# First tokens of a fused Fourier mixer and MLP in another order, stores on GpSimd's queue, weight conversions rescheduled

## The chip, the cores and the metric

One core of a Trainium2 chip runs the whole kernel. The metric is device microseconds of one launch. Several executions are timed; their median counts. One more execution is profiled, and all rows below are from that one.

## The reference

`x` has 8 batches of 3072 positions and 256 channels. Each batch is mixed along its positions in the frequency domain, and the result goes through a two-layer MLP, all in float32:

```
X = rfft(x, axis=1)
Yr = Xr @ w_r - Xi @ w_i + b_r          # 256 x 256 weights
Yi = Xr @ w_i + Xi @ w_r + b_i
Y = soft_shrink(Yr, 0.01) + 1j * soft_shrink(Yi, 0.01)
x = irfft(Y, n=3072, axis=1).reshape(8 * 3072, 256)
h = x @ w_in                            # 256 x 2048
out = softplus(h) @ w_out               # 2048 x 256
```

## The kernel before

Large matmuls are made of three: every operand is split into a high and a low part in fp32r, and `mm3` (L207 to L210) adds high x high, high x low and low x high. A batch passes through these stages:

- `s1` (16 chunks c per batch): a short Fourier transform over 96 rows, psf, copied by ACT (L260). In the early part the chunks of batch 0 stay on the chip as `a0`; chunks of batch 1 go to DRAM (`a_dr`) and come back as `ap` (L273 to L276).
- `s3`, the mix and `s4` for 12 groups gp: the second transform (L287), the product with w_r and w_i (`wmh`, `wml`), bias and soft shrinkage on DVE and POOL (z, cl; L377 to L382), the first step back (L427), copied as `d` (L432) and stored to `d_dr`.
- `s5`: the last step of the inverse transform. The tokens come as four blocks (column block j, channel half k) from `dp`, which is read from `d_dr` (L440, L441). `b11`, `b21`, `b12`, `b22` make from them the seven left factors of a Strassen-like product (`whole`, `keep`, `difference`, `split_token`; L474 to L489).
- The MLP, by a key (batch, pair of blocks, slice m2 of the hidden units): seven products psc and pse by the seven combinations of `w_in`, sums on ACT and DVE (L532, L537), softplus (L543), splitting (L547, L553), and pso with `w_out`.

**Weights.** `w_in` and `w_out` arrive as 64-bit numbers. A generator `split_w` converts one piece j of 16 (load L143; L158 to L194 on ACT, DVE and POOL) and stores it to DRAM (L195), from where `stream_w` (L204) loads it for each key. A piece is spread over several steps, one part at each `yield`: L158 to L161 first, then L163 to L165, then the sum (L178 to L182), the cast L192, the low part L194 and the store. The pieces with `early` set that belong to `w_in` use a corner of the buffer `y1`; all others share one buffer, `wp` (`bufs=1`). So the next piece's L178 or L182 waits until the last store from `wp` has landed.

**Order.** The program is written out step by step. A list `first` gives the steps before zero (`early` is on): s1 of batch 0, the 12 groups with s1 of batch 1 in between, then six more s1 of batch 1 (c = 4 to 9), then four s5. From step 0 on there are four steps per key. `at(t, f, ...)` hangs a piece of work (a load, a conversion, an s1) on step t; `later` puts off something by one step, and `store` (L97) uses it. SyncE's queue (SP) issues nearly all DMAs in that order; one that has to wait holds all behind it. Buffers count: `x`, `xh`, `xl`, `a`, `d` and the streamed weights have two each, the early `xt` lie in the buffers of `gh` and `gl`.

What the change touches: `store` (L97), `load_w` (L137), `split_w` (L150 to L196), `load_x` (L225), `s1` (L240 to L264), `s5` (L445 to L462), `put_split` and `b12` to `b21` (L493 to L516), and the schedule (L646 to L718).

Of the kernel before, what the change touches and what calls it, by code (L numbers as in the profile page):

```python
# [10 lines left out]
F32 = mybir.dt.float32  # L11
# [3 lines left out]
ALU = mybir.AluOpType  # L15

B, S, D, DFF = 8, 3072, 256, 2048
P = 128
# [3 lines left out]
BLK = 512  # L22
# [11 lines left out]
def tile_spectral_mixer_mlp(ctx, tc, x, w_r, w_i, bias, bias_0, w_in, w_out, f, f_hi, f_lo, g1, g3, g3_hi, g3_lo, hm, out):  # L34
# [61 lines left out]

    def store(dst, src, what):  # L97

        def start():
            nc.sync.dma_start(dst, src)  # L100
            stored[what] += 1

        later.append(start)
# [33 lines left out]
    def load_w(which, m2):  # L137

        if m2 < 6:
            st = sb.tile([P, 1024 + 4 * N1], F32, tag="dp", name="w64", bufs=4)[:, :1024]  # L140
        else:
            st = sb.tile([P, 1024], F32, tag="w64", name="w64", bufs=1)
        nc.sync.dma_start(st.rearrange("p (a n) -> p a n", a=2).bitcast(U32), (w_in if which else w_out)[:, m2])  # L143
        stages[which, m2] = st

    def split_w(which, m2):
# [46 lines left out]
        yield  # L193
        v.tensor_tensor(out=lo, in0=src, in1=hi.bitcast(F32), op=ALU.subtract)  # L194
        nc.sync.dma_start((w1_dr if which else w2_dr)[m2][:, :], w.bitcast(F32))  # L195
        stored["w", which, m2] += 1  # L196
# [28 lines left out]
    def load_x(b, c):  # L225

        if b == 0 or (b, c // 10) == (1, 0):
            xt = sb.tile([P, 512], F32R, tag=("gh", "gl")[c % 2], name="xt", bufs=3).bitcast(F32)[:N1]
        else:
            xt = sb.tile([P, 512], F32, tag="x", name="xt", bufs=2)[:N1]  # L230
        nc.sync.dma_start(
            xt.rearrange("p (n c) -> p n c", n=2),
            x[b].rearrange("(p n) c -> p n c", n=N2)[:, 2 * c:2 * c + 2, :],
        )
        xs[b, c] = xt
# [7 lines left out]
    def s1(b, c):  # L243
# [17 lines left out]
        if b == 0:  # L261
            stored["a", b] += 1
        else:
            store(a_dr[b][:, 2 * c:2 * c + 2, :].rearrange("(g q) n c -> q g n c", q=4), a.rearrange("p (n c) -> p n c", n=2), ("a", b))  # L264

# [182 lines left out]
    def s5(b, blk, k):  # L448
# [3 lines left out]
        while t < (blk + 1) * BLK:  # L452
# [8 lines left out]
            t += n  # L461
        (b11, b21, b12, b22)[blk % 2 * 2 + k]((b, blk // 2), ps)  # L462

# [29 lines left out]
    def put_split(*args):  # L493
        split_token(*args) if early else later.append(lambda: split_token(*args))

# [7 lines left out]
    def b12(key, ps):  # L503
        difference(0, ps)
        keep(key, 1, ps)
        put_split(key, T1, 0, nc.vector if early else nc.gpsimd)

    def b22(key, ps):
        whole(key, B22, ps)
        difference(1, ps)  # L510
        difference(0, ps)
        put_split(key, T2, 0, nc.vector if early else nc.gpsimd)
        put_split(key, T3, 1, nc.vector)

    def b21(key, ps):
        whole(key, B21, ps)  # L516
        difference(0, ps)
        put_split(key, T4, 0, nc.vector if early else nc.gpsimd)

# [107 lines left out]
    with tc.manual_schedule():  # L627
# [17 lines left out]
        def plan_s1(b, start, step, first=0):  # L645
            for c in range(first, 16):  # L646
                t = product(start + step * (c - first), s1, b, c)
                at(t - 3, split_x, b, c)
                at(t - 7, load_x, b, c)

# [28 lines left out]

        first += [("s1", 1, c) for c in range(4, 10)]  # L680
        first += [("s5", j, k) for j, k in ((0, 0), (1, 0), (1, 1), (0, 1))]
        t0 = -len(first)
# [17 lines left out]
        for k in range(2):  # L700
            at(t0 + 14 + k, load_mix, k)
            at(t0 + 18 + k, split_mix, k)
        for j in range(NM):
            t = t0 + 23 + 5 * j if j < 9 else 1 + 3 * (j - 9)
            at(t - (6 if j < 9 else 4 if j < 12 else 2), load_w, (j + 1) % 2, j // 2)
            before.setdefault(t, []).append(split_w((j + 1) % 2, j // 2))
# [10 lines left out]
        nt = NT  # L717
        plan_s1(1, 1, 1.6, 10)  # L718
        for b in range(B):
# [135 lines left out]
```

## Time and profile before

| | |
|---|---|
| median of the runs | 2680.17 us |
| lowest and highest of 3 | 2677.96 and 2680.23 us |
| the profiled execution: its own time | 2679.82 us |
| its span in the trace | 2678.0 us |
| PE busy | 2603.8 us, 97% of the span |
| DVE, ACT, POOL busy | 61%, 64%, 11% |
| mean granted clock of TensorE | 0.987 |

The span is what the trace covers; 1.8 us of the profiled execution's time lie around it. Shares are means over the whole span, most of which is the steady part from step 24 on. What differs is the start, so the sections below look at stretches of the first 250 us. Lines (L195) are those of the code printed above; `w_dr` in the trace stands for the arrays `w1_dr` and `w2_dr`, `w` for several weight tiles, and `a_dr<-y` for the early chunks of batch 1 that are kept in `y1`.

### The profile page before, as it was taken

How to read it: one execution, taken by the hardware profiler on the slowest of the kernel's cores; microseconds unless marked ns; L12 is line 12 of the kernel's file. 1: busy time of each engine (PE TensorE's matmuls, PEld its weight loads, DVE VectorE, ACT ScalarE, POOL GpSimd, SP SyncE). 2: the span in 40 equal slices, each digit the busy share in tenths (PEclk: the TensorE clock that was granted, in tenths of full speed). 3: DMA queues.
4: the chain of work that ended last, by engine and by line, in shares of the span. 5: the costliest groups of instructions: out<-in, count | busy, mean ns of one | idle time of the engine just before them, and what ended most of it. 6: DMA issues, size and time to landing. Idle time of an engine off the chain costs nothing.

```text
span 2678.0 us, 36264 instructions
## 1 busy us (share of the span) xinstructions
PE 2603.8 (97%) x13059; PEld 2184.2 (82%) x13059; DVE 1626.2 (61%) x2701; ACT 1719.5 (64%) x3115; POOL 301.3 (11%) x292
## 2 busy tenths in 40 slices
PE   7768999999999999999999999999999999999999
PEld 5546888888888888888888888888888888888887
DVE  3666665666646666566665666556665666645454
ACT  3365666666666666666676666666666666666665
POOL 2432110110101101101011011010010000000000
PEclk8889999999999999999999999999999999999999
DMA  6766556556455565564555644646455455445543
GB/s 191 254 210 206 194 164 198 166 187 193 157 188 178 178 198 170 179 205 156 184 172 172 217 159 153 220 163 198 164 167 191 155 170 188 142 154 183 186 147 110
DMA packets 186116, 479.73 MB, mean 179 GB/s; under 512 B 18097, under 2 KB 86961, under 8 KB 185937
## 3 DMA queue, kind: packets, MB, share of 16 engines
q1 hardware_dynamic: 185376, 476.95, 55.1%
q8 instruction: 103, 1.69, 0.3%
q0 software_dynamic: 560, 0.47, 0.1%
q14 instruction: 77, 0.62, 0.1%
HBM read 390.31 MB, written 83.89 MB: 177 GB/s over the span
## 4 chain that ended last, share of the span: by engine, by line
PE 88%; DVE 2%; DMA 2%; ACT 1%; issue 0%; POOL 0%; SPq 0%; DVEq 0%; ACTq 0%; POOLq 0%
PE pso L208 13%; PE pso L209 12%; PE pso L210 12%; PE psc L208 6%; PE psc L210 6%; PE psc L209 6%; PE pse L208 5%; PE pse L210 5%; PE pse L209 5%; PE psf L455 4%; PE psf L209 4%; PE psf L208 4%; PE psf L210 4%; PE psf L287 2%; DMA w_dr<-wp 1%; DVE shrunk L413 0%
## 5 line engine op out<-in xcount | busy, mean ns | idle before, releaser
L553 DVE TENSOR_TENSOR gl<-t,gh 128x512 fp32r<-128x512 f32 x768 | 533.2, 694 | 349.7 <-ACT gh L547 346.8
L532 ACT COPY t<-psc 128x512 f32<-128x512 f32 x576 | 337.0, 585 | 504.4 <-PE psc L210 502.4
L537 DVE TENSOR_TENSOR t<-pse,t 128x512 f32<-128x512 f32 x576 | 396.2, 688 | 426.9 <-ACT t L532 278.3
L208 PE MATMUL pso<-gh,w 128*128 128x512 f32 x1536 | 616.2, 401 | 0.0
L209 PE MATMUL pso<-gl,w 128*128 128x512 f32 x1536 | 600.0, 391 | 0.0
L210 PE MATMUL pso<-gh,w 128*128 128x512 f32 x1536 | 599.5, 390 | 0.0
L547 ACT CAST gh<-t 128x512 fp32r<-128x512 f32 x768 | 476.8, 621 | 58.2 <-PE pso L210 34.4
L543 ACT ACTIVATE t<-t 128x512 f32<-128x512 f32 x576 | 364.5, 633 | 58.7 <-DVE t L537 58.0
L210 PEld LDWEIGHTS pso<-gh,w 128*128 128x128 f32 x1536 | 288.7, 188 | 62.5
L208 PEld LDWEIGHTS pso<-gh,w 128*128 128x128 f32 x1536 | 290.1, 189 | 54.9
L209 PEld LDWEIGHTS pso<-gl,w 128*128 128x128 f32 x1536 | 290.0, 189 | 51.4
L208 PE MATMUL psc<-y_sb,w 128*128 128x512 f32 x768 | 301.6, 393 | 16.1 <-DMA w<-w_dr 7.8
L210 PE MATMUL psc<-y_sb,w 128*128 128x512 f32 x768 | 300.1, 391 | 0.0
L209 PE MATMUL psc<-y_sb,w 128*128 128x512 f32 x768 | 299.6, 390 | 0.0
L208 PE MATMUL pse<-y_sb,w 128*128 128x512 f32 x576 | 227.8, 396 | 14.4 <-DVE t L537 7.9
L115 POOL TENSOR_TENSOR xl<-xt,xh 96x512 fp32r<-96x512 f32 x102 | 134.1, 1317 | 938.3 <-ACT xh L106 783.6
L209 PE MATMUL pse<-y_sb,w 128*128 128x512 f32 x576 | 225.2, 391 | 0.0
L210 PE MATMUL pse<-y_sb,w 128*128 128x512 f32 x576 | 225.1, 391 | 0.0
L489 POOL TENSOR_TENSOR y_sb<-raw,y_sb 128x512 fp32r<-128x512 f32 x69 | 92.3, 1337 | 1128.5 <-ACT y_sb L486 1124.9
L208 PEld LDWEIGHTS psc<-y_sb,w 128*128 128x128 f32 x768 | 144.5, 188 | 51.0 <-ACT t L532 10.2
L210 PEld LDWEIGHTS psc<-y_sb,w 128*128 128x128 f32 x768 | 144.6, 188 | 31.0
L209 PEld LDWEIGHTS psc<-y_sb,w 128*128 128x128 f32 x768 | 144.6, 188 | 29.7
(131 smaller groups left out, 3637.8 us busy)
## 6 DMA issues: line engine op xcount, KB each, us to landing
w<-w_dr SPq DMA_DIRECT2D x192, 896.0 KB
w<-w_dr SPq DMA_DIRECT2D x192, 512.0 KB
dp<-d_dr SPq DMA_DIRECT2D x80, 384.0 KB
xt<-in_x SPq DMA_DIRECT2D x128, 192.0 KB
d_dr<-d SPq DMA_DIRECT2D x96, 256.0 KB
out_y<-ot SPq DMA_DIRECT2D x96, 256.0 KB
ap<-a_dr SPq DMA_DIRECT2D x84, 256.0 KB
a_dr<-a SPq DMA_DIRECT2D x102, 192.0 KB
```

The costliest lines, as they stand in the source:

```text
L115: (eng or nc.vector).tensor_tensor(out=lo, in0=src, in1=hi.bitcast(F32), op=ALU.subtract)
L208: nc.tensor.matmul(ps, wh, xh, start=start, stop=False, skip_group_check=more)
L209: nc.tensor.matmul(ps, wh, xl, start=False, stop=False, skip_group_check=more)
L210: nc.tensor.matmul(ps, wl, xh, start=False, stop=stop, skip_group_check=more)
L287: nc.tensor.matmul(xv[:, g, k], t[:, g, k * P:(k + 1) * P], g1_t[:, g].rearrange("p (c s) -> p c s", c=2), start=True, stop=True,)
L455: nc.tensor.matmul(ps[:, t - blk * BLK:t - blk * BLK + n], d_sb[b, blk // 2, n2 // 4][0][:, n2 % 4, k * P:(k + 1) * P], d_sb[b, blk // 2, ...
L489: eng.tensor_tensor(out=lo, in0=raw[j], in1=hi.bitcast(F32), op=ALU.subtract)
L532: nc.scalar.copy(t, banks[bank])
L537: nc.vector.tensor_tensor(out=t, in0=banks[bank], in1=t, op=ALU.add)
L543: nc.scalar.activation(t, banks[bank] if bank else t, AF.Softplus)
L547: nc.scalar.copy(gh, ct[key, what])
L553: nc.vector.tensor_tensor(out=gl, in0=ct.pop((key, what)), in1=gh.bitcast(F32), op=ALU.subtract)
```

## The change

- `first_tokens` makes the first tokens in the order of its s5: (0,0), (0,1), (1,0), (1,1). B11 and B21 come first; the others after the last s5; T4 a step later.
- Eight chunks of batch 1 are made ahead instead of ten (c = 4 to 7 after the groups); the other eight are planned from step 0 on, 1.3 steps apart (steps 0, 1, 2, 3, 5, 6, 7, 9; before, six at 1, 2, 4, 5, 7, 9), and loaded five steps ahead instead of seven.
- The early chunks' stores to `a_dr` go by GpSimd's queue.
- Eight pieces (j below 8) are converted ahead, one place earlier in the list, instead of nine. From j = 8 on a piece begins at step 3(j - 8): for j = 9 and up that is two steps later than before.
- A piece's store stands one `yield`, so one step, behind its low part.
- w_r and w_i are loaded five places earlier.

```diff
@@ -94,10 +94,10 @@
     def put_off(f):
         later.append(f) if early else f()
-    def store(dst, src, what):
+    def store(dst, src, what, eng=None):
         def start():
-            nc.sync.dma_start(dst, src)
+            (eng or nc.sync).dma_start(dst, src)
             stored[what] += 1
         later.append(start)
@@ -136,7 +136,7 @@
     def load_w(which, m2):
-        if m2 < 6:
+        if m2 < 6 and (which, m2) != (1, 4):
             st = sb.tile([P, 1024 + 4 * N1], F32, tag="dp", name="w64", bufs=4)[:, :1024]
         else:
             st = sb.tile([P, 1024], F32, tag="w64", name="w64", bufs=1)
@@ -192,6 +192,7 @@
         nc.scalar.copy(hi, src)
         yield
         v.tensor_tensor(out=lo, in0=src, in1=hi.bitcast(F32), op=ALU.subtract)
+        yield
         nc.sync.dma_start((w1_dr if which else w2_dr)[m2][:, :], w.bitcast(F32))
         stored["w", which, m2] += 1
@@ -224,7 +225,7 @@
     def load_x(b, c):
-        if b == 0 or (b, c // 10) == (1, 0):
+        if b == 0 or (b, c // 8) == (1, 0):
             xt = sb.tile([P, 512], F32R, tag=("gh", "gl")[c % 2], name="xt", bufs=3).bitcast(F32)[:N1]
         else:
             xt = sb.tile([P, 512], F32, tag="x", name="xt", bufs=2)[:N1]
@@ -261,7 +262,8 @@
         if b == 0:
             stored["a", b] += 1
         else:
-            store(a_dr[b][:, 2 * c:2 * c + 2, :].rearrange("(g q) n c -> q g n c", q=4), a.rearrange("p (n c) -> p n c", n=2), ("a", b))
+            store(a_dr[b][:, 2 * c:2 * c + 2, :].rearrange("(g q) n c -> q g n c", q=4), a.rearrange("p (n c) -> p n c", n=2), ("a", b),
+                  nc.gpsimd if early else None)
     def load_a(b, gp):
         assert stored["a", b] == 16
@@ -459,7 +461,10 @@
                 start=True, stop=True,
             )
             t += n
-        (b11, b21, b12, b22)[blk % 2 * 2 + k]((b, blk // 2), ps)
+        if early:
+            first_tokens((b, blk // 2), blk % 2 * 2 + k, ps)
+        else:
+            (b11, b21, b12, b22)[blk % 2 * 2 + k]((b, blk // 2), ps)
@@ -491,7 +496,32 @@
         low() if early or eng is nc.gpsimd else later.append(low)
     def put_split(*args):
-        split_token(*args) if early else later.append(lambda: split_token(*args))
+        later.append(lambda: split_token(*args))
+
+    def first_tokens(key, i, ps):
+
+        v = nc.vector
+        if i == 0:
+            b11(key, ps)
+        elif i == 1:
+            whole(key, B21, ps)
+            raw[2] = sb.tile([P, BLK], F32, tag="d", name="raw")
+            nc.scalar.copy(raw[2], ps)
+        elif i == 2:
+            b12(key, ps)
+        else:
+            difference(0, ps)
+            difference(1, ps)
+            for j, t in ((0, T2), (1, T3)):
+                nc.scalar.copy(tokens(key, t)[0], raw[j])
+            nc.scalar.copy(tokens(key, B22)[0], ps)
+            for j, t in ((0, T2), (1, T3)):
+                hi, lo = tokens(key, t)
+                v.tensor_tensor(out=lo, in0=raw[j], in1=hi.bitcast(F32), op=ALU.subtract)
+            hi, lo = tokens(key, B22)
+            v.tensor_tensor(out=lo, in0=ps, in1=hi.bitcast(F32), op=ALU.subtract)
+            v.tensor_tensor(out=raw[2], in0=raw[2], in1=raw[0], op=ALU.subtract)
+            put_split(key, T4, 2, v)
     def b11(key, ps):
@@ -503,19 +533,19 @@
     def b12(key, ps):
         difference(0, ps)
         keep(key, 1, ps)
-        put_split(key, T1, 0, nc.vector if early else nc.gpsimd)
+        (split_token if early else put_split)(key, T1, 0, nc.vector if early else nc.gpsimd)
     def b22(key, ps):
         whole(key, B22, ps)
         difference(1, ps)
         difference(0, ps)
-        put_split(key, T2, 0, nc.vector if early else nc.gpsimd)
+        put_split(key, T2, 0, nc.gpsimd)
         put_split(key, T3, 1, nc.vector)
     def b21(key, ps):
         whole(key, B21, ps)
         difference(0, ps)
-        put_split(key, T4, 0, nc.vector if early else nc.gpsimd)
+        put_split(key, T4, 0, nc.gpsimd)
     gt, po, ct, banks = {}, {}, {}, {}
@@ -646,7 +676,7 @@
             for c in range(first, 16):
                 t = product(start + step * (c - first), s1, b, c)
                 at(t - 3, split_x, b, c)
-                at(t - 7, load_x, b, c)
+                at(t - (5 if b == 1 else 7), load_x, b, c)
         def plan_mix(b, start, step):
             mixed = done = start
@@ -677,8 +707,8 @@
             if 1 <= i <= NP:
                 first.append(("mix", 0, i - 1))
-        first += [("s1", 1, c) for c in range(4, 10)]
-        first += [("s5", j, k) for j, k in ((0, 0), (1, 0), (1, 1), (0, 1))]
+        first += [("s1", 1, c) for c in range(4, 8)]
+        first += [("s5", j, k) for j, k in ((0, 0), (0, 1), (1, 0), (1, 1))]
         t0 = -len(first)
         for t, (what, b, i) in enumerate(first, t0):
             if what == "s1":
@@ -698,11 +728,11 @@
         at(t0 + 18, nc.sync.dma_start, bias0, bias_0)
         at(-6, nc.sync.dma_start, bias_sb, bias)
         for k in range(2):
-            at(t0 + 14 + k, load_mix, k)
+            at(t0 + 9 + k, load_mix, k)
             at(t0 + 18 + k, split_mix, k)
         for j in range(NM):
-            t = t0 + 23 + 5 * j if j < 9 else 1 + 3 * (j - 9)
-            at(t - (6 if j < 9 else 4 if j < 12 else 2), load_w, (j + 1) % 2, j // 2)
+            t = t0 + 22 + 5 * j if j < 8 else 3 * (j - 8)
+            at(t - (6 if j < 8 else 8 if j < 9 else 4 if j < 12 else 2), load_w, (j + 1) % 2, j // 2)
             before.setdefault(t, []).append(split_w((j + 1) % 2, j // 2))
         last = first.index(("s4", 0, NP - 1)) + t0
         for c in need_d(0):
@@ -715,7 +745,7 @@
             at(6 + 2 * k, combine_mix, 1 + k)
         nt = NT
-        plan_s1(1, 1, 1.6, 10)
+        plan_s1(1, 0, 1.3, 8)
         for b in range(B):
             for bp in range(1, NPAIR):
                 plan_s5(b, bp, nt * b + 2 * NM * bp - 14)
```

The line numbers in the orders below are those of each kernel; the changed one has its `ap` loads at L275 for L273, its z at L379 for L377, its stores of weights at L196 for L195.

SyncE's queue while the groups begin: w_216 and w_204 are the same piece of `w_in`, bias_99 is the bias, `a_79` is `a0`. Before:

```order
L273 DMA ap<-a_79 128x1x256 x6
L143 DMA w_216<-in_w_in 128x2x512
L100 DMA a_dr<-y_80 4x24x512
L273 DMA ap<-a_79 128x1x256 x2
L749 DMA bias_99<-in_bias 128x512
L100 DMA a_dr<-y_80 4x24x512 x3
L273 DMA ap<-a_79 128x1x256 x2
```

After, the queue from the same weight load on:

```order
L143 DMA w_204<-in_w_in 128x2x512
L275 DMA ap<-a_79 128x1x256 x8
L779 DMA bias_99<-in_bias 128x512
L275 DMA ap<-a_79 128x1x256 x2
L143 DMA w_255<-in_w_out 128x2x512
L779 DMA y_80<-in_g 128x1536
```

The store to `a_dr` is gone from between the weight load and the bias. It and the three behind it are issued by GpSimd, right behind its first load:

```order
L663 DMA g_sb<-in_g 128x256
L100 DMA a_dr<-y_80 4x24x512 x4
L319 COPY real<-w_239 128x256
L321 MEMSET real 128x2 x2
L319 COPY real<-w_239 128x256
```

VectorE at the last two groups, where z is the step before `s4`: `wp` is the sixth piece converted. Before:

```order
L377 TENSOR_TENSOR z<-psf,bias_99 128x512
L381 TENSOR_SCALAR cl<-z 128x512
L159 TENSOR_SCALAR wt<-w_792 128x512
L160 SCALAR_TENSOR_TENSOR wt<-w_792,wt 128x512
L377 TENSOR_TENSOR z<-psf,bias_99 128x512
L381 TENSOR_SCALAR cl<-z 128x512
L163 SCALAR_TENSOR_TENSOR wt<-wu,wt 128x512
L164 TENSOR_SCALAR wu<-wt 128x512
L194 TENSOR_TENSOR wp<-wp 128x512
```

After:

```order
L379 TENSOR_TENSOR z<-psf,bias_99 128x512
L383 TENSOR_SCALAR cl<-z 128x512
L159 TENSOR_SCALAR wt<-w_784 128x512
L160 SCALAR_TENSOR_TENSOR wt<-w_784,wt 128x512
L163 SCALAR_TENSOR_TENSOR wt<-wu,wt 128x512
L164 TENSOR_SCALAR wu<-wt 128x512
L194 TENSOR_TENSOR wp<-wp 128x512
L379 TENSOR_TENSOR z<-psf,bias_99 128x512
L383 TENSOR_SCALAR cl<-z 128x512
```

L163, L164 and L194 of that piece now stand ahead of the last z and cl.

SyncE's queue in steps 0 to 7: w_dr_85 is the ninth piece's store (j = 8), w_dr_93 the tenth's; a load w_dr_83 fetches a converted piece of 896 KB. Before:

```order
L231 DMA xt<-in_x 96x512
L100 DMA a_dr<-a 4x24x512
L195 DMA w_dr_85<-y_80 128x1792
L143 DMA w_1191<-in_w_out 128x2x512
L204 DMA w_1193<-w_dr_90 128x1024
L100 DMA a_dr<-a 4x24x512
L204 DMA w_1239<-w_dr_83 128x1792
L195 DMA w_dr_93<-wp 128x1024
```

After:

```order
L232 DMA xt<-in_x 96x512
L100 DMA a_dr<-a 4x24x512
L205 DMA w_1197<-w_dr_90 128x1024
L100 DMA a_dr<-a 4x24x512
L232 DMA xt<-in_x 96x512
L205 DMA w_1236<-w_dr_83 128x1792
L100 DMA a_dr<-a 4x24x512
L196 DMA w_dr_85<-wp 128x1792
L143 DMA w_1271<-in_w_out 128x2x512
L100 DMA a_dr<-a 4x24x512
```

The ninth piece's store comes from `wp` and stands behind a load of xt, the 896 KB and three stores to `a_dr`; before it came from `y1` and stood ahead of all but one.

## Rows read from the trace of the kernel before

**Rows 1.** The busy time by stage: start and end, length, busy us of PE, PE's weight loads, DVE, ACT and POOL (instructions in brackets), the granted clock of TensorE, the busy share of the DMA engines, GB/s.
```profile
0.00:250.00 250.00, 187.09 (x852) 140.56 (x853) 141.88 (x243) 116.97 (x211) 79.02 (x81) 0.86 0.66 216
49.50:106.00 56.50, 49.38 (x333) 42.09 (x331) 51.47 (x82) 24.66 (x47) 33.33 (x28) 0.97 0.70 234
157.70:250.00 92.30, 71.91 (x309) 56.12 (x310) 57.67 (x106) 52.12 (x93) 22.41 (x21) 0.92 0.66 224
250.00:2678.00 2428.00, 2416.71 (x12208) 2043.61 (x12207) 1484.29 (x2460) 1602.49 (x2905) 222.31 (x211) 1.00 0.54 175
```

**Rows 2.** The timeline of all engines from 28 us on, a few rows of it: start, duration, engine, line and operation; in square brackets the idle time ahead and what ended it. SPq is SyncE's DMA issue.
```profile
28.06 1.25 SPq L143 DMA_DIRECT2D w<-in_w_in  x1
...
29.41 0.66 SPq L100 DMA_DIRECT2D a_dr<-y  x1
...
32.58 2.35 SPq L749 DMA_DIRECT2D bias<-in_bias  x1
...
41.52 0.69 DVE L380 TENSOR_TENSOR z<-psf,bias 128x512 f32<-128x512 f32 x1 [9.19 <-DMA bias<-in_bias]
...
43.41 0.58 PE L210 MATMUL psf<-wmh,w 128*128 128x256 f32 x1 [4.77 <-DVE w L115]
...
48.27 1.65 PE L287 MATMUL psf<-y,ap 128*128 128x128 f32 x8
...
50.43 0.47 PE L208 MATMUL psf<-wmh,w 128*128 128x256 f32 x1
...
53.49 1.06 PE L287 MATMUL psf<-y,ap 128*128 128x128 f32 x8
```

**Rows 3.** The table by stretch for two stretches of four microseconds, columns as in rows 1.
```profile
26.00:30.00 4.00, 2.06 (x8) 1.79 (x8) 0.38 (x1) 0.00 (x0) 0.00 (x0) 0.50 0.28 97
20.00:24.00 4.00, 3.58 (x9) 1.13 (x7) 0.11 (x1) 2.98 (x6) 0.00 (x0) 1.00 0.86 293
```

**Rows 4.** The timeline of all engines from 100 to 120 us, columns as in rows 2.
```profile
101.50 0.43 SPq L100 DMA_DIRECT2D d_dr<-d  x1
...
104.09 0.68 DVE L163 SCALAR_TENSOR_TENSOR wt<-wu,wt 128x512 f32<-128x512 f32 x1
...
105.95 1.12 PE L427 MATMUL psf<-z,g_sb 128*128 128x512 f32 x2 [2.21 <-POOL z L382]
...
106.10 0.68 DVE L194 TENSOR_TENSOR wp<-wp 128x512 fp32r<-128x512 f32 x1
...
106.81 0.33 SPq L195 DMA_DIRECT2D w_dr<-wp  x1
...
107.70 0.58 ACT L432 COPY d<-psf 128x512 f32<-128x512 f32 x1 [3.29 <-DMA d_dr<-d]
...
108.43 0.93 SPq L100 DMA_DIRECT2D d_dr<-d  x2
...
119.88 0.50 PE L455 MATMUL psf<-dp 96*128 96x96 f32 x1 [5.95 <-DMA dp<-d_dr]
```

**Rows 5.** The timeline of all engines from 119 to 158 us, PE's rows where it waited or changed its work.
```profile
131.07 0.77 PE L208 MATMUL psc<-y_sb,w 128*128 128x512 f32 x1
...
139.20 0.79 PE L208 MATMUL pse<-y_sb,w 128*128 128x512 f32 x1 [6.50 <-ACT y_sb L474]
...
142.18 0.79 PE L208 MATMUL psc<-y_sb,w 128*128 128x512 f32 x1 [1.03 <-ACT t L532]
...
143.62 0.63 PE L208 MATMUL pse<-y_sb,w 128*128 128x512 f32 x1
...
144.90 0.48 PE L208 MATMUL psf<-xh,fh 96*96 96x512 f32 x1
...
145.69 0.40 PE L208 MATMUL psc<-y_sb,w 128*128 128x512 f32 x1
...
157.72 0.77 PE L208 MATMUL psc<-y_sb,w 128*128 128x512 f32 x1 [7.14 <-DMA w<-w_dr]
```

**Rows 6.** The waits of all engines from 157.7 to 250 us: engine and line, what they waited for, us in total, times, the longest.
```profile
DVE wp L178 <- DMA w_dr<-wp: 10.1, 2, 8.4
...
ACT raw L479 <- DVE y_sb L475: 9.2, 1, 9.2
...
DVE wp L182 <- DMA w_dr<-wp: 6.0, 3, 3.1
...
ACT wu L158 <- DMA w<-in_w_in: 4.6, 2, 2.5
```

**Rows 7.** The timeline of all engines from 212 to 230 us, columns as in rows 2.
```profile
216.49 0.32 SPq L195 DMA_DIRECT2D w_dr<-wp  x1
...
225.40 0.42 DVE L178 TENSOR_TENSOR wp<-wt,wu 128x256 f32<-128x256 f32 x1 [8.37 <-DMA w_dr<-wp]
...
228.56 0.58 PE L208 MATMUL psf<-wmh,lh 128*128 128x256 f32 x1 [5.93 <-ACT raw L479]
```

**Rows 8.** Groups of instructions by line, 0 to 260 us: line, engine, operation, tiles and count, busy us, mean ns of one, idle time ahead and what ended it.
```profile
L165 POOL TENSOR_TENSOR wu<-w,wu 128x512 f32<-128x512 f32 x16 | 27.9, 1742 | 103.1 <-DVE wu L164 51.7 <-DMA w<-w_dr 12.9 <-ACT t L543 8.8
...
L115 POOL TENSOR_TENSOR xl<-xt,xh 96x512 fp32r<-96x512 f32 x8 | 11.7, 1471 | 2.5 <-ACT xh L106 2.5
```

**Rows 9.** The waits of SyncE's DMA queue from 0 to 270 us, columns as in rows 6.
```profile
SPq L195 <- DVE wp L194: 67.6, 9, 19.5
...
SPq L231 <- POOL xl L115: 17.8, 3, 8.5
```

## The prediction

> **What bounds the kernel now.** The table by stage comes first [rows 1]: look at PE's busy time against the length of each stretch. From 250 us on PE works 2416.71 of 2428.00 us at full clock; before that it works 187.09 of 250 us. After the start TensorE is the bound, nothing in the change removes matmuls, and every term below is therefore a wait in the first 250 us that goes, shrinks or appears. I then followed four places in the timelines, and the tables of waits for what repeats.
>
> At 27 to 45 us [rows 2]: PE stands still for 4.77 us before 43.41, because DVE has to read psf first and is itself held 9.19 us by the load of the bias, issued at 32.58 behind a weight load (28.06), a store to `a_dr` (29.41) and `ap` loads. While they run, the DMA engines are busy 0.28 of the time and move 97 GB/s, where six microseconds earlier it was 0.86 and 293 GB/s [rows 3]; four partitions wide, they look as if they used 4 of 16 engines. After the pause 22 small matmuls run at half clock: 4.86 us, from 43.41 to 48.27.
>
> At 100 to 120 us [rows 4]: the last product s4 is at 105.95, but SP stands in front of the last two `d_dr` stores until DVE's L194 at 106.10 lets the converted weight out, and ACT's copy of d is held 3.29 us by an earlier `d_dr` store. The `d_dr` stores go at 108.43, and the tokens' matmuls (s5), which need them back as `dp`, begin at 119.88. From there to 157.72 [rows 5]: waits of 6.50 us (B21 ready last), 1.03 and 7.14 us (a weight load that SP issued late).
>
> From 157.7 to 250 us PE is idle for 20.4 of 92.3 us [rows 1]; the table of waits [rows 6] shows DVE held by its single `wp` buffer (10.1 + 6.0 us behind stores), ACT held by DVE for raw (9.2) and by weight loads (4.6). The worst instance [rows 7]: a store issued at 216.49 lands so late that DVE's L178 starts at 225.40, and PE waits 5.93 us.
>
> **The change, term by term.** All sums are against the profiled execution, 2679.82 us (the median of the runs is 2680.17, 0.35 more, which I neglect).
>
> *A, the bias.* The first `a_dr` store now leaves SP's row ahead of the bias: 192 KB at 97 GB/s, an estimate of 2.0 us on those engines. The weight load of 512 KB and w_r, w_i go in earlier: 512 KB at 293 GB/s [rows 3] is 1.8 us. Together 3.8 of the 4.77 us that PE waits. Then TensorE's clock need not fall from its upper level to its lower: the 22 matmuls took 4.86 us, while 24 took 3.06 at the full clock, from 50.43 to 53.49 [rows 2]; 22 of those are 2.8, so 2.0 us more. That makes 5.8; I take -5.5 us, since DVE has little room up to 106 us (51.47 of 56.5 us busy [rows 1]). The lower bound is a loss: if the four stores on GpSimd's queue share the same engines and come ahead, three more stand in front of the bias than now (3 x 2.0 = 6 us, less 1.8): +4. Upper: -6.8 (all 4.77 and the clock's 2.0).
>
> *B, the last stores of d.* L163, L164 and L194 of the sixth conversion now stand ahead of the last z on DVE, so SP is no longer held by L194 from 101.93 (101.50 and 0.43) to 106.81 [rows 4], and ACT's copy of d loses its wait of 3.29. In exchange that z comes 2.7 us later (the three fill DVE from 104.09 to 106.78), and with it s4, the last copy and its store: 110.5 instead of 108.43, with the wait of 3.29 gone and the store tied to the copy alone. From the store to s5 it took 11.5 us (108.43 to 119.88), with a weight load of 896 KB issued just before and one of 512 KB just after. Freed of L194, SP issues the 896 KB some 4.9 us sooner, and their 3.1 us (at 293 GB/s, [rows 3]) no longer lie in front; the 512 KB (1.8 us) stand in front instead of between store and load, half of them run by then: 0.9 less. So 110.5 + 11.5 - 3.1 - 0.9 = 118: taken -2. Bounds +2 (the loads are still in the way) and -4. Two s1 products that no longer stand between only lengthen PE's wait for dp: 0, as long as dp is the last to come.
>
> *C, from s5 to step 4.* Before, 26.65 us from the end of s5 (131.07) to step 4 (157.72), of which 14.7 are the three waits of [rows 5]. Gone: all of these (B21 is computed second, and SP is free to issue the load). Added: two more s1 products in steps 0 to 3; the trio of one took 0.79 us at 144.90, the trio ahead of it 1.28 at half clock, so 1.1 each: 2.2. And new waits on ACT, which has one order: xh of chunk 10 now stands ahead of the copy for C11 and needs the s1 of chunk 8, which PE makes later (one trio at half clock, 1.3 us); xh of chunk 11 in the same way ahead of a softplus (two trios and the cast, 3); the copy of a for chunk 10 needs `a_dr` of chunk 8 stored, and that store stands on SP behind a load of xt that waits for POOL's xl behind POOL's L165: 1.47 and 1.74 us [rows 8] and the store's 2.0, 5 in all. So 26.65 - 14.7 + 2.2 + 9.3 = 23.45: taken -3.2. Bounds -8 (half of the new waits are covered) and -1.
>
> *D, step 7.* The ninth conversion (j = 8) no longer writes the early buffer y but `wp`, and its store, a step later, stands on SP behind xt of chunk 15, a weight load of 896 KB and an `a_dr` store; the tenth conversion writes `wp` only when it has landed. Now SP waits 17.8 us in three cases for POOL's xl and 67.6 us in nine for DVE's L194 [rows 9], so such a row is no hypothesis. xl and L165, the load's 3.1 us and the store's own 3.1 make 9.4, against nothing before at that place; less some slack DVE is held 6 to 9 us, of which PE sees about 0.7, as in [rows 7] (8.37 us of DVE, 5.93 of PE). Taken: +5. Bounds 0 (the xt loads come early) and +10.
>
> *E, the other six conversions.* Same wait, same buffer, each store behind the loads of the next step (512 KB and 896 KB: 1.8 and 3.1 us at 293 GB/s). Before, five such landings cost DVE 16.1 us [rows 6]; each can grow by 0 to 4. Paid back: weight loads come earlier for ACT (4.6 us [rows 6]). Net 0; bounds -4 and +7. Moved s1 products of batch 1 beyond step 9 fill PE all the same: 0.
>
> **Sum:** -5.5 - 2 - 3.2 + 5 + 0 = -5.7, and 2679.82 - 5.7 = 2674.1. Every bound at its good end gives 2657 (-6.8 - 4 - 8 + 0 - 4), every one at its bad end 2702 (+4 + 2 - 1 + 10 + 7); neither is likely.
>
> **Rivals.** A measurement can tell 0.2% (5.4 us) from no change; faster means under 2674.8, slower over 2685.5.
>
> *Slower: the single `wp` buffer decides (2687).* D at its bad end (+10) and E at +7 (a store behind loads each time), with A to C, -10.7 as taken, at -10: 2679.8 + 17 - 10 = 2687. It decides from the point where a store lands more than some 2 us after DVE reaches the next write of `wp`, the slack that DVE shows beside PE in a step. For it: the case of [rows 7], where a store needed 8.9 us to land while loads were ahead of it, and putting it later puts more ahead. Against: the four other landings cost 3.1 us or less each [rows 6].
>
> *Level: 2680.* ACT's row gets no cheaper: the waits that I count as 9.3 in C come to 12.5, as much as is removed net of the s1 products, and D and E cost 7.5 where A and B win 7.5. For it: the first 250 us are a chain of buffers of two, where time gained early is given back at the next free buffer.
>
> *More gain: 2665.* D does not come (0), C is at -6, A and B are as taken and E gives 1.5: -15. For it: a load that stood behind a store held by DVE's L194 (67.6 us of such waits, [rows 9]) now goes ahead of it and is in time.
>
> *The stores on GpSimd's queue do not clear the way: 2680 to 2684.* No row of this trace shows a 4-partition store from that queue. If they use the same four engines as `ap` and come in between, A is 0 to +4, and the rest is -0.2. This is the case in which the change doesn't do what it says for the bias. For it: `ap` and `a_dr` have the same narrow shape. Against: only that the queue is another one.
>
> Two rules of the Trainium skill bear on this rival, from either side. "DMA: Bandwidth & Descriptors", section "Why a DMA increments its semaphore by 16 and not by 1": a transfer is spread over the most engines, up to 16, that divide its slowest dimensions; from a hardware queue those are the lowest-numbered ones, from GpSimd's they go round. The quarter share of [rows 3] agrees with the first half; no run here shows the second, by which this rival falls away and A stands. "SBUF — State Buffer", section "SBUF: two separate sides": descriptors of such a DMA are written by GpSimd's cores, which are locked out while VectorE runs in a two-port mode; by it the stores come late once DVE works again, out of the bias's way but in that of later `ap` loads.
>
> **Chances.** Forecast 0.40 (its own range 2667 to 2679: 0.28 faster, 0.12 same). Slower rival 0.24 (0.20 slower, 0.04 same). Level 0.12 (0.10 same, 0.01 on either side). More gain 0.14 (faster). GpSimd's queue 0.10 (0.06 same, 0.03 slower, 0.01 faster). Sums: faster 0.44, same 0.32, slower 0.24. As range I take 2663 to 2690: from just past the larger gain to just past the slower rival, with the bad ends of A, D and E together left outside.
>
> **What would show it.** A: z first at about 38 us and PE without the 4.8 us pause, no half clock there. B: s5 begins some 7.5 us earlier (about 112). C: no wait of 6 us before the first pse, step 4 about 23 us after the end of s5, and ACT waiting on xh and a. D: a DVE wait of 6 us or more on a `w_dr` store in steps 5 to 7. E: waits of DVE on `w_dr` of 16 us or more in all. From 250 us on nothing: PE there as busy as now. I am wrong if s5 begins no earlier, if DVE's waits on `w_dr` double, or if after 250 us PE shows new gaps.

## The result and the profile after

The changed kernel takes 2699.92 us (median of 6 runs, 2698.13 to 2700.74) against 2680.20 us of the kernel before beside it: a ratio of 1.0072, 95% interval 1.0059 to 1.0085. It is 19.7 us slower where 5.7 us of gain were forecast. The profiled execution took 2700.74 us, its span is 2699.0.

The table by stage of the changed kernel, columns as in [rows 1]:

```profile
0.00:250.00 250.00, 179.09 (x789) 134.57 (x790) 131.47 (x218) 109.45 (x196) 83.20 (x86) 0.83 0.63 200
157.70:250.00 92.30, 65.25 (x244) 50.98 (x245) 50.98 (x87) 47.30 (x83) 24.85 (x22) 0.80 0.56 183
250.00:300.00 50.00, 44.97 (x229) 38.57 (x228) 36.85 (x67) 29.78 (x57) 8.63 (x6) 0.90 0.57 187
300.00:2699.00 2399.00, 2387.62 (x12046) 2018.17 (x12044) 1460.72 (x2420) 1584.27 (x2867) 217.66 (x207) 1.00 0.55 175
```

The steady part, from 300 us on, is as full as before. The start is not: by 250 us PE has been busy 179.09 us instead of 187.09, and the stretch from 157.7 to 250 us has lost most (65.25 instead of 71.91, at a granted clock of 0.80 instead of 0.92). The end of the disturbed part moved from 250 to some 270 us.

Most useful is a table that the profile only gives indirectly: when each step begins, read as the start of its first psc matmul in PE's timeline (us).

| step | before | changed | difference | forecast of the difference |
|---|---|---|---|---|
| 0 (end of s5) | 131.07 | 131.17 | +0.1 | -7.5 (A, B) |
| 4 | 157.72 | 158.84 | +1.1 | -10.7 (with C) |
| 8 | 173.54 | 189.33 | +15.8 | -5.7 (with D) |
| 16 | 205.46 | 216.32 | +10.9 | |
| 24 | 252.39 | 273.12 | +20.7 | -5.7 (with E) |
| 30 | 276.07 | 296.81 | +20.7 | |

After step 24 the difference stays. So in this profile the start gave nothing, steps 4 to 8 lost 14.7 us, and steps 8 to 24 another 4.9.

How the 20.6 us between step 0 and step 24 show on PE: the same table for that stretch, first the kernel before, then the changed one.

```profile
131.07:252.39 121.32, 86.01 (x356) 65.44 (x357) 77.83 (x139) 69.01 (x125) 33.48 (x31) 0.87 0.61 206
131.17:273.12 141.95, 99.48 (x363) 76.72 (x363) 81.62 (x141) 70.91 (x127) 35.24 (x30) 0.77 0.54 176
```

PE stands idle 7.2 us longer (42.5 for 35.3), but it is also busy 13.5 us longer, at a granted clock of 0.77 instead of 0.87. The two s1 trios that moved in are 1.6 to 2.6 us of that (0.79 and 1.28 each, [rows 5]). By estimate the other 11 us or so are matmuls that ran at the lower of the two clock levels: behind the wait of 5.32 us at 158.84 a psc matmul takes 0.63 us, at 173.35 it takes 0.40. The prediction prices the clock in A and in its s1 trios, and nowhere for the waits that it adds.

**The first group, against [rows 2].** The timeline of all engines of the changed kernel from 26 to 46 us (start, duration, engine, line, operation, and in brackets the idle time ahead and its cause):

```profile
27.32 0.68 PE L289 MATMUL psf<-y,ap 128*128 128x128 f32 x4 [2.52 <-issue]
...
30.74 1.23 PE L289 MATMUL psf<-y,ap 128*128 128x128 f32 x4 [2.74 <-DMA ap<-a]
...
35.23 1.20 PE L289 MATMUL psf<-y,ap 128*128 128x128 f32 x4 [3.27 <-DMA ap<-a]
35.75 1.46 SPq L779 DMA_DIRECT2D bias<-in_bias  x1
...
43.16 0.69 DVE L382 TENSOR_TENSOR z<-psf,bias 128x512 f32<-128x512 f32 x1 [8.10 <-DMA bias<-in_bias]
...
45.05 0.39 PE L211 MATMUL psf<-wmh,w 128*128 128x256 f32 x1 [2.50 <-DVE w L115]
```

The bias is issued later than before (35.75 against 32.58), and z comes at 43.16 instead of 41.52. PE's waits for `ap` are 2.74 and 3.27 us here, behind 2.52 put down to issue; from 20 to 60 us they come to 6.4 us in all, and to 5.1 in the kernel before. The stores from 20 to 45 us (KB each, us from issue to landing, median):

```profile
a_dr<-y POOLq DMA_DIRECT2D x4, 192.0 KB, 11.2
```

The DMA queues from 28 to 32 us (packets, MB, share of 16 engines):

```profile
q0 software_dynamic: 304, 0.55, 57.6%
q1 hardware_dynamic: 84, 0.08, 11.4%
```

The kernel before from 26 to 30 us, where almost only `ap` loads run:

```profile
q1 hardware_dynamic: 389, 0.39, 28.1%
```

Four stores of 192 KB from GpSimd's queue (q0) land 11.2 us after their issue. Once the weight load ahead of them is done, from 28 to 32 us, they take 57.6% of the 16 engines' time, so more than four engines. The `ap` loads beside them (q1) get 84 packets through in four microseconds, where alone they got 389.

**The last stores of d, against [rows 4] and [rows 5].** The same kernel from 102 to 124 us:

```profile
106.53 1.37 PE L429 MATMUL psf<-z,g_sb 128*128 128x512 f32 x2 [3.33 <-POOL z L384]
...
108.60 0.36 SPq L100 DMA_DIRECT2D d_dr<-d  x1
...
118.27 1.99 PE L457 MATMUL psf<-dp 96*128 96x96 f32 x8 [5.48 <-DMA dp<-d_dr]
...
122.64 1.56 PE L457 MATMUL psf<-dp 96*128 96x96 f32 x6 [2.38 <-DMA dp<-d_dr]
```

s5 begins at 118.27 instead of 119.88, as B had it (118 without A). But its second part waits 2.38 us more for `dp`, where before it was 0.68, and both kernels end s5 within 0.1 us.

**Steps 0 to 24, against [rows 6].** The waits of all engines from 131 to 275 us (us in total, times, longest):

```profile
DVE wp L182 <- DMA w_dr<-wp: 22.3, 4, 9.5
PE pse L209 <- DVE t L567: 21.6, 6, 7.4
...
PE psc L209 <- ACT t L562: 15.6, 6, 5.0
...
ACT a L261 <- DMA a_dr<-a: 11.4, 2, 8.1
DVE wp L178 <- DMA w_dr<-wp: 9.3, 2, 6.5
```

DVE waits 31.6 us for landings of converted weights. In the kernel before, the same two lines gave 16.1. Beside them stands ACT, held 11.4 us by stores to `a_dr` (3.4 before). The worst case, in the timeline from 166 to 186 us:

```profile
169.22 1.08 DVE L194 TENSOR_TENSOR wp<-wp 128x896 fp32r<-128x896 f32 x1
...
172.72 0.33 SPq L232 DMA_DIRECT2D xt<-in_x  x1
...
173.15 0.36 SPq L205 DMA_DIRECT2D w<-w_dr  x1
...
174.28 0.42 SPq L196 DMA_DIRECT2D w_dr<-wp  x1
...
182.78 0.69 DVE L182 TENSOR_TENSOR wp<-wt,wu 128x512 f32<-128x512 f32 x1 [9.54 <-DMA w_dr<-wp]
...
184.13 0.80 PE L209 MATMUL pse<-y_sb,w 128*128 128x512 f32 x1 [7.38 <-DVE t L567]
```

The low part of the ninth piece is ready at 170.30 (169.22 and 1.08). Its store goes at 174.28, behind a load of xt and a weight load that SP issued at 172.72 and 173.15. It lands 8.5 us later; L182 is held for 9.54 us, PE for 7.38. That is D as described: DVE is held 9.54 us where the sum had 6 to 9, and PE 7.38 where it had 5.

### The profile page after: what moved, and what is told of

Same layout as the page of the kernel before. It is cut to its first block, busy times and chain, and to the rows that moved or that the text cites. A ratio compares the mean times of both kernels' runs of the same rounds, so it can differ in the third digit from the quotient of the medians.

```text
span 2699.0 us, 36284 instructions
## 1 busy us (share of the span) xinstructions
PE 2611.7 (97%) x13061; PEld 2191.3 (81%) x13061; DVE 1629.0 (60%) x2704; ACT 1723.5 (64%) x3118; POOL 309.5 (11%) x299
## 4 chain that ended last, share of the span: by engine, by line
PE 88%; DVE 2%; DMA 1%; ACT 1%; issue 1%; POOL 0%; SPq 0%; DVEq 0%; POOLq 0%; ACTq 0%
PE pso L209 13%; PE pso L210 12%; PE pso L211 12%; PE psc L209 6%; PE psc L211 6%; PE psc L210 6%; PE pse L209 5%; PE pse L211 5%; PE pse L210 5%; PE psf L457 4%; PE psf L210 4%; PE psf L211 4%; PE psf L209 4%; PE psf L289 2%; DMA w_dr<-wp 1%
## 5 line engine op out<-in xcount | busy, mean ns | idle before, releaser
L573 ACT ACTIVATE t<-t 128x512 f32<-128x512 f32 x576 | 364.4, 633 | 57.6 <-DVE t L567 56.7
```

Of the source, the lines that this page charges most:

```text
L573: nc.scalar.activation(t, banks[bank] if bank else t, AF.Softplus)
```

## The experiments

Twelve kernels; the table gives the median, the ratio to the kernel before with its 95% interval, and the start of steps 0, 4, 8 and 24 in the profile (before: 131.07, 157.72, 173.54, 252.39).

| kernel | us | ratio, interval | step 0 | 4 | 8 | 24 |
|---|---|---|---|---|---|---|
| changed | 2699.92 | 1.0072 [1.0059, 1.0085] | 131.17 | 158.84 | 189.33 | 273.12 |
| e1: changed, no added yield | 2694.73 | 1.0054 [1.0037, 1.0071] | 130.03 | 160.48 | 187.01 | 266.93 |
| e2: changed, a_dr stores on SP | 2696.20 | 1.0059 [1.0044, 1.0074] | 125.62 | 154.66 | 186.80 | 270.55 |
| e3: before, the yield alone | 2701.75 | 1.0077 [1.0062, 1.0092] | 132.25 | 160.30 | 174.37 | 272.94 |
| e4: before, GpSimd's stores alone | 2680.16 | 1.0000 [0.9991, 1.0009] | 132.41 | 155.22 | 173.03 | 250.39 |
| e5: changed, late weight stores on ACT's queue | 2692.75 | 1.0038 [1.0025, 1.0051] | 125.75 | 153.27 | 179.22 | 263.18 |
| e7: before, the token order alone | 2680.79 | 1.0001 [0.9992, 1.0010] | 130.23 | 157.00 | 173.06 | 251.76 |
| e8: changed, no yield, old plan of s1 | 2672.41 | 0.9970 [0.9958, 0.9981] | 130.21 | 150.80 | 166.50 | 245.75 |
| e9: before, the new plan of s1 alone | 2685.53 | 1.0020 [1.0011, 1.0029] | 133.26 | 156.97 | 177.65 | 258.85 |
| e10: e8 with a_dr stores on SP | 2673.08 | 0.9974 [0.9964, 0.9985] | 128.70 | 150.66 | 165.94 | 244.00 |
| e11: changed, old plan of s1 | 2676.94 | 0.9989 [0.9980, 0.9998] | 128.90 | 146.23 | 165.43 | 249.22 |
| e12: before, the schedule of conversions alone | 2675.09 | 0.9982 [0.9973, 0.9992] | 129.23 | 152.01 | 167.46 | 247.49 |
| e13: before, yield, two buffers | 2680.98 | 1.0002 [0.9993, 1.0011] | 131.01 | 159.21 | 174.42 | 253.94 |

One caution with the columns at the right: they are one profile each. e5 issues the same instructions as the changed kernel up to step 0 and reaches it at 125.75 instead of 131.17. Up to 5 us at step 0 are therefore not read as an effect; the medians are.

**e1, the yield taken out of the changed kernel.**

```diff
         v.tensor_tensor(out=lo, in0=src, in1=hi.bitcast(F32), op=ALU.subtract)
-        yield
         nc.sync.dma_start((w1_dr if which else w2_dr)[m2][:, :], w.bitcast(F32))
```

> The changed kernel with the conversion's store issued in the step of its low part again (the added yield gone), all else as changed. Theory 1 (the later store, behind loads on SP, is most of the loss): 2699.9 - 13 or more, so 2680 to 2688; DVE's waits on w_dr stores, 31.6 us between 157.7 and 275 us, fall to 18 or less. Theory 2 (the other parts, schedule of conversions and s1 or GpSimd's stores, make the loss): 2694 or more, waits hardly changed.

Measured: 2694.73 us, 5.2 less. The time is that of theory 2, the waits are those of theory 1: DVE's fell to 14.6 us, and yet the time hardly. What took their place, in the waits from 131 to 275 us:

```profile
ACT a L260 <- DMA a_dr<-a: 19.9, 3, 10.0
...
DVE wp L182 <- DMA w_dr<-wp: 7.3, 4, 2.6
DVE wp L178 <- DMA w_dr<-wp: 7.3, 1, 7.3
```

ACT now waits 19.9 us for stores to `a_dr`. One of the three, in the timeline from 146 to 162 us:

```profile
146.79 1.63 POOL L165 TENSOR_TENSOR wu<-w,wu 128x512 f32<-128x512 f32 x1 [8.46 <-ACT a L260]
...
148.38 1.29 POOL L115 TENSOR_TENSOR xl<-xt,xh 96x512 fp32r<-96x512 f32 x1
...
149.70 0.32 SPq L231 DMA_DIRECT2D xt<-in_x  x1
...
150.08 0.66 SPq L100 DMA_DIRECT2D a_dr<-a  x1
...
157.66 0.58 ACT L260 COPY a<-psf 96x512 f32<-96x512 f32 x1 [9.97 <-DMA a_dr<-a]
...
160.48 0.79 PE L208 MATMUL psc<-y_sb,w 128*128 128x512 f32 x1 [8.48 <-ACT t L572]
```

Read it backwards. PE waits 8.48 us for a softplus on ACT. ACT stands in the copy of a, which needs a buffer whose store SP issued only at 150.08, right behind a load of xt. That load waited for POOL's xl at 148.38, and this stood behind POOL's L165, itself held 8.46 us by ACT. The store then took 7 us to land. This is the chain that C named, with 9.97 us where the sum had 5, and it comes back at 167.24 (4.15) and 184.18 (5.75), which the sum had not.

**e2, the early stores on SP's queue again in the changed kernel.**

```diff
-                  nc.gpsimd if early else None)
+                  None)
```

> The changed kernel with the early stores to a_dr on SP's queue again, all else as changed. Theory 1 (later stores of weights are the loss): 2696 to 2700, only the start is better by 0 to 4 us. Theory 2 (stores on GpSimd's queue meet the ap loads on the same four engines and delay all that follows): 2690 to 2695, and the first group starts 4 us earlier (at 33 instead of 37.7 us).

Measured: 2696.20 us, 3.7 less (2694.29 to 2697.33, below all six executions of the changed kernel), but e4 and e10 below find nothing for the same edit. Step 0 comes 5.5 us sooner, but no sooner than in e5 (125.75), which has these stores on GpSimd's queue.

**e3, the yield alone in the kernel before** (the one line of e1, added).

> The kernel before with the added yield alone. Theory 1: slower by 8 to 16 us, 2688 to 2696, with DVE's waits on w_dr between 157.7 and 250 us grown from 16.1 to 25 or more. Rival (the yield hurts only with the new schedule of conversions, where the ninth piece too writes wp): 2678 to 2684.

Measured: 2701.75 us, 21 more than before, by the yield alone, and above the range of theory 1. DVE's waits, 131 to 275 us:

```profile
DVE wp L178 <- DMA w_dr<-wp: 21.2, 3, 8.6
...
DVE wp L182 <- DMA w_dr<-wp: 17.0, 3, 13.6
```

38.2 us in place of 16.1. The largest, in the timeline from 210 to 232 us:

```profile
212.05 1.08 DVE L194 TENSOR_TENSOR wp<-wp 128x896 fp32r<-128x896 f32 x1
...
214.32 0.38 SPq L143 DMA_DIRECT2D w<-in_w_in  x1
...
218.24 0.58 SPq L442 DMA_DIRECT2D dp<-d_dr  x1
...
218.93 0.63 SPq L196 DMA_DIRECT2D w_dr<-wp  x1
...
229.03 0.69 DVE L182 TENSOR_TENSOR wp<-wt,wu 128x512 f32<-128x512 f32 x1 [13.58 <-DMA w_dr<-wp]
...
231.32 0.79 PE L209 MATMUL pse<-y_sb,w 128*128 128x512 f32 x1 [12.10 <-DVE t L538]
```

The low part is ready at 213.13. In that step SP has a weight load, which waits for POOL, and eight loads for the next tokens; the store goes behind them all at 218.93, lands ten microseconds later, and PE stands 12.10 us. In the changed kernel the pieces fall on other steps, and the store that meets these token loads goes ahead of them (214.02 against 214.45). The same yield costs less there, 5 us; that this is why is likely and not shown.

**e4, GpSimd's stores alone in the kernel before.**

```diff
-            store(a_dr[b][...].rearrange(...), a.rearrange(...), ("a", b))
+            store(a_dr[b][...].rearrange(...), a.rearrange(...), ("a", b),
+                  nc.gpsimd if early else None)
```

> The kernel before with the early stores to a_dr on GpSimd's queue alone (ten stores). Theory (same four engines as the ap loads): the first group 4 us later than the 33.25 us of before, given back by DVE's bound stretch in part: +1 to +4, so 2681 to 2684. Rival (as forecast: the bias comes sooner): 2674 to 2678.

Measured: 2680.16 us, no difference within 0.1%. PE's waits for `ap` between 20 and 60 us:

```profile
PE psf L288 <- DMA ap<-a: 10.2, 4, 4.7
```

Before they were 5.1 us in three. So the stores do get into the way of the `ap` loads, and yet nothing of it is left in the time. The first z shows the same in all the kernels: it comes at 40.3 to 41.9 us in the eight with these stores on SP's queue, and at 41.9 to 45.0 in the six with them on GpSimd's. The forecast of A (-5.5) has no support: the queue neither brought the bias forward nor cost time in the end.

**e7, the order of the tokens alone** (`first_tokens` and its s5, put into the kernel before).

> The kernel before with the new order of the first tokens alone. Theory (the new order works by itself): the wait of 6.50 us before the first pse goes, step 1 starts 4 to 5 us earlier; the wait for the weight load before step 4 (7.14 us) stays and takes it back at least in part: 2675 to 2680. Rival (the order costs ACT more than it saves): 2682 or more.

Measured: 2680.79 us, no difference. PE's timeline from 130 to 158 us, the rows with a wait over 1 us:

```profile
139.88 0.80 PE L208 MATMUL psc<-y_sb,w 128*128 128x512 f32 x1 [6.46 <-ACT t L560]
...
157.00 0.77 PE L208 MATMUL psc<-y_sb,w 128*128 128x512 f32 x1 [6.62 <-DMA w<-w_dr]
```

The wait of 6.50 us for B21 is gone, but 6.46 us before step 1 wait for ACT instead, since the first sums now share ACT with the tokens that are left; and the weight load before step 4 is as late as ever (6.62). The gain of 2.3 us at step 1 is 0.7 at step 4.

**e8, the changed kernel without the yield and with the old plan of batch 1's s1.**

```diff
-        first += [("s1", 1, c) for c in range(4, 8)]
+        first += [("s1", 1, c) for c in range(4, 10)]
-        plan_s1(1, 0, 1.3, 8)
+        plan_s1(1, 1, 1.6, 10)
```

with the old buffers of xt for chunks 8 and 9 and loads seven steps ahead.

> The changed kernel without the added yield and with the old plan of batch 1's s1 (ten ahead, six later, their loads and buffers as before). It differs from the run without the yield (2694.7) by that plan alone. Theory 3 (making eight ahead leaves chunks 8 to 15 to a narrow chain: two buffers of a, x and xh, with SP in order between them): 2676 to 2684, ACT's waits for a_dr stores fall from 19.9 to 6 us or less, step 8 starts at most 3 us after the 173.5 of before. Rival (the conversions moved later make it): 2690 or more.

Measured: 2672.41 us, 22.3 less than e1, from which it differs by the plan alone. The waits from 131 to 275 us:

```profile
DVE wp L182 <- DMA w_dr<-wp: 9.4, 4, 3.3
...
DVE wp L178 <- DMA w_dr<-wp: 6.6, 1, 6.6
ACT a L260 <- DMA a_dr<-a: 6.4, 3, 3.4
```

ACT's waits for `a_dr` fell from 19.9 to 6.4. This kernel is faster than both, by 7.8 us against the one before, and faster than theory 3 had it.

**e9, the new plan of s1 alone in the kernel before.**

> The kernel before with the new plan of batch 1's s1 alone (eight ahead, eight from step 0 on, loads five steps ahead); nine conversions ahead at the same distance from step 0 as before. Theory 3: 2688 to 2698, with ACT waiting 12 us or more for a_dr stores between 131 and 200 us. Rival (conversions): 2678 to 2684.

Measured: 2685.53 us, 5.3 more. The direction is that of theory 3, the size was too high: with the old conversions the plan costs a quarter of what it costs with the new ones (22.3).

**e5, the late weight stores on ScalarE's queue, changed kernel.**

```diff
-        nc.sync.dma_start((w1_dr if which else w2_dr)[m2][:, :], w.bitcast(F32))
+        (nc.sync if ahead else nc.scalar).dma_start((w1_dr if which else w2_dr)[m2][:, :], w.bitcast(F32))
```

> The changed kernel with the late conversions' stores (j of 8 and up) issued by ScalarE's queue instead of SP's, still a step after their low part. If SP's order is what makes them late (issue 2 to 4 us after the low part, and behind its loads): 2686 to 2694, DVE's waits on w_dr fall from 31.6 to 20 us or less. If the landing itself is slow because of the loads in flight: 2697 to 2702, waits 27 or more.

Measured: 2692.75 us, 7.2 less. The waits from 131 to 275 us:

```profile
ACT a L261 <- DMA a_dr<-a: 16.7, 3, 8.1
...
DVE wp L178 <- DMA w_dr<-wp: 11.6, 3, 5.7
...
DVE wp L182 <- DMA w_dr<-wp: 9.4, 4, 3.7
```

DVE's two lines give 21.0 in place of 31.6, so a third of the wait was the store's place on SP's queue. ACT's waits for `a_dr` remain, 16.7 us instead of 11.4: nothing in the plan of s1 was touched.

**e11, the fourth corner: the yield with the old plan of s1.**

> The changed kernel, added yield kept, with the old plan of batch 1's s1. Fourth corner of a square of yield and plan (both 2699.9, plan alone 2694.7, neither 2672.4). If the two add up: 2677 to 2680. If either alone spoils the same stretch (the yield alone cost the old kernel 21): 2688 to 2697.

Measured: 2676.94 us. All four corners have the new tokens, conversions and queue:

| | old plan of s1 | new plan | the plan costs |
|---|---|---|---|
| no yield | 2672.41 | 2694.73 | 22.3 |
| yield | 2676.94 | 2699.92 | 23.0 |
| the yield costs | 4.5 | 5.2 | |

The two add up here. The starts of the steps, from the table above, show where each is paid (us added; one profile each):

| | steps 0 to 4 | 4 to 8 | 8 to 24 |
|---|---|---|---|
| the plan, yield kept (e11 to changed) | +10.3 | +11.3 | 0.0 |
| the plan, no yield (e8 to e1) | +9.9 | +10.8 | +0.7 |
| the plan, in the kernel before (before to e9) | -2.9 | +4.9 | +2.4 |
| the yield, new plan (e1 to changed) | -2.8 | +4.0 | +3.9 |
| the yield, old plan (e8 to e11) | -3.3 | +3.5 | +4.5 |

**e12, the schedule of conversions alone in the kernel before** (eight ahead, one place earlier; from j = 8 at step 3(j - 8); the loads with it).

> The kernel before with the new schedule of conversions alone (eight ahead, one place earlier, j of 8 and up at step 3(j - 8), their loads as in the change; no added yield, old tokens, old s1, old queue). If it is this part that gains in the 2672.4 us kernel: 2671 to 2677. If it gains only together with the new order of the tokens (the weight load before step 4 then comes in time, and the tokens no longer wait): 2678 to 2684.

Measured: 2675.09 us, 5.0 less. This part gains by itself. The wait for weights between 131 and 275 us:

```profile
PE psc L208 <- DMA w<-w_dr: 3.8, 2, 2.8
```

Before it was 7.14 us in one wait, at step 4 [rows 5]. Step 4 now begins at 152.01, 5.7 us sooner, and 4.9 of them are left at step 24.

**e10, e8 with the early stores on SP's queue again** (the edit of e2).

> The kernel of 2672.4 us (changed, without the added yield, old plan of s1) with the early stores to a_dr on SP's queue again. If GpSimd's stores cost what their removal gave on the changed kernel (3.7 us): 2666 to 2670. If they are neutral, as they were on the kernel before (0.0): 2671 to 2674.

Measured: 2673.08 us against 2672.41: neutral, as in e4.

**e13, the yield alone with a second place for the converted pieces**, up to j = 13 (the pieces of `w_in` in the early corner of `y1`, those of `w_out` in `wp`).

```diff
-        w = w_1 if early and which else sb.tile([P, 2 * 7 * P], F32R, tag="wp", name="wp", bufs=1)
+        w = w_1 if which and (early or m2 < 7) else sb.tile([P, 2 * 7 * P], F32R, tag="wp", name="wp", bufs=1)
```

> The kernel before with the added yield, and with two buffers for the converted pieces in place of one up to j = 13: the pieces of w_in use the early corner of y1 until step 18, those of w_out use wp. If the single buffer is what makes the later store costly: 2679 to 2688 instead of 2701.8, and DVE's waits on w_dr from 38 us to under 10 (j = 14 and 15 still share wp). If it is the loads and stores changing places on SP: 2696 or more.

Measured: 2680.98 us: the whole 21 us of the yield are gone, with the store still a step late and in the same place on SP. DVE's waits, 131 to 275 us:

```profile
DVE wp L178 <- DMA w_dr<-wp: 12.8, 1, 12.8
...
DVE wp L182 <- DMA w_dr<-wp: 0.8, 1, 0.8
```

They come to 13.6 us, not under 10. The 12.8 us are at a piece that still shares `wp` (226.67), and PE stands 9.01 us behind it, where it stood 5.93 before [rows 7]. For the yield in the kernel before, the single buffer is the mechanism, shown by taking it away.

## Why the prediction was wrong

The 19.7 us are: 23 from the plan of batch 1's s1, 5 from the store a step later, and -8 from what is left. Of these the schedule of the conversions makes 5 by itself, the tokens and the queue nothing that can be told; the earlier load of w_r and w_i was not tried alone. The split holds for the changed kernel. In the kernel before, the plan alone costs 5 (e9) and the store 21 (e3).

- **The step that failed is C.** It let the cost of the new plan of s1 end at step 4. For steps 0 to 4 it priced that plan at 11.5 us (2.2 of work, 9.3 of waits), and the traces show 10; for steps 4 to 8 the sum has no term for it, and the traces show 11 more (table at e11). The chain xl, xt, `a_dr`, copy of a was named rightly, POOL's L165 included [rows 8], but it was priced once, at 5 us. Chunks 8 to 15 all pass through it, with two buffers each, so it comes back up to step 8: 9.97, 4.15 and 5.75 us in e1, 8.08 and 3.32 in the changed kernel. The 14.7 us that C took off were too much as well: with the old plan, steps 0 to 4 take 17.33 us (e11) and 20.59 (e8), so 9.3 and 6.1 less than before. The six chunks of the old plan pass the same two buffers with 6.4 us of waiting. Whether it is the two more chunks, their closer distance (1.3 steps for 1.6) or the later loads (five steps ahead for seven) that fills these buffers, no run separates.
- **A** was wrong altogether. The bias was issued 3.2 us later, and z came 1.6 us later instead of 3.8 sooner, behind `ap` loads that the stores held up, and the gain rested on the stores leaving SP's queue, without a row for a store from GpSimd's. The rival that the stores don't clear the way had the right effect and the wrong reason: these stores took more than the four engines of the `ap` loads (57.6% of 16, from 28 to 32 us). That agrees with the rule of the Trainium skill, "DMA: Bandwidth & Descriptors", section "Why a DMA increments its semaphore by 16 and not by 1", that such a queue's transfers go round the engines. That they then leave the `ap` loads alone, as the prediction took from it, does not hold, by the 10.2 us of e4.
- **B** named the time for s5 (118.27 against 118) by luck. The last store of d went at 108.60, not 110.5, and s5 followed 9.7 us behind it, not 7.5, so two misses cancel; e5, with the same instructions up to there, has s5 at 115.20. B also missed that the second wait for `dp` would be 1.7 us longer.
- **D** was right in place, mechanism and about in size: DVE 9.54 and PE 7.38 in the trace, at a clock of 0.80 in this stretch, and 3.5 to 4.0 us in steps 4 to 8 by the yield taken out, where the sum had 5. With it out, ACT's copy of a holds PE at the same place (5.32 us before step 8 in e1). The rest of the 14.7 us that steps 4 to 8 lost is C's chain.
- **E** had the sign open (-4 to +7) and 0 in the sum; the yield costs 3.9 to 4.5 us there. DVE's waits doubled, 16.1 to 31.6, as the slower rival had it, of which the ninth piece is 9.54. The condition in that rival ("more than some 2 us after DVE reaches the next write") was met at five of the six landings up to 275 us and was not weighed: from the `yield` alone one can read that the store now falls in the same step as the next write of a single buffer, so that its whole way to DRAM becomes a wait. Before, it had a step.

The rival that named 2687 used the right mechanism for the smaller part of the loss. No case had both that and ACT's chain in full, and the range ended at 2690.

What stays open: why the plan of s1 costs 22 us with the new conversions and 5 with the old (e9). The table at e11 says where: most of the difference is in steps 0 to 4, where the kernel before waits 7.14 us for a weight load at step 4 [rows 5], a wait that e9 no longer has. In these steps ACT waits 2.7 us for an `a_dr` store in e9 and 9.97 in e1: in e9 the first L165 after step 0 comes behind the xl on which that store hangs (152.43 against 146.61), in e1 ahead of it (146.79 against 148.38). That the place of this L165 is the cause is likely, but no run moves it alone.

## What to carry to other kernels

A store that empties a single buffer must be issued as soon as it can be: a step's delay costs its landing, not the delay, and here landings took 8 to 10 us with loads ahead of them (174.28 to 182.78 in the changed kernel, 218.93 to 229.03 in e3). When work is moved out of a prologue into steps, count the buffers of each stage that it passes and walk the in-order queues for every piece that goes through them, not for the first one. And of several edits that belong together, time each: of the five timed here one was worth 5 us, two nothing, and two cost 28. But a price found with one edit alone need not be its price in the whole: plan and store cost 23 and 5 us in the changed kernel, and 5 and 21 in the one before.

## What the runs showed of the hardware

A store of 192 KB over four partitions from GpSimd's queue leaves 208 packets where SP's leaves 100: eight of them add 1664 to q0 and take 800 from q1. But 160 of the 208 are only 4 or 8 bytes long; the data go in 48 packets of 4096 bytes, from SP's queue in 96 of 2048. The first four landed in 11.2 us (median) in the changed kernel and in 7.4 in e5, with `ap` loads in flight. In that time the narrow loads of SP's queue fell to 84 packets in four microseconds, from 389 alone. And two executions of the same instructions can stand 5 us apart at 130 us (e5 and the changed kernel), although no instruction differs up to there; the six executions of the changed kernel lie within 2.6 us.
